# The first MLP block of a fused attention and two-MLP kernel, issued in another order

## The chip, the cores and the metric

The kernel runs on one core of a Trainium2 chip. The metric is the device time of one execution in microseconds (us); lower is better.

## The reference

Delta-rule attention over 768 steps for 4 batches and 8 heads of 48, then a PReLU MLP (384 to 2048 to 384), then a SiLU-gated MLP (384 to 1536 to 384), all on the same 3072 tokens:

```python
for t in range(S):
    y[:, :, t] = np.einsum('bhd,bhde->bhe', q[:, :, t], state)
    v_old = np.einsum('bhde,bhd->bhe', state, kt)          # kt: k / (|k| + 1e-6)
    state = state + bt[..., None] * np.einsum('bhd,bhe->bhde', kt, vt - v_old)
x = y.transpose(0, 2, 1, 3).reshape(B * S, H * D)
h = x @ w_in;  g = np.maximum(h, 0) + alpha * np.minimum(h, 0);  x = g @ w_out
g = x @ w_gate;  out = (g / (1 + np.exp(-g)) * (x @ w_val)) @ w_out2
```

The weights and alpha come as float64.

## The kernel before

The attention is computed in 24 chunks of 32 steps (`NCH`), four chunks to a window. A chunk c goes through six pieces of small products on TensorE: `do_KS` (state against k, tile pk; VectorE then subtracts it from v), `do_QS` (state against q, tile py), `do_U` (tile pu; ScalarE copies U out), `do_S` (the state's update, pst; VectorE adds it to St), `do_Y` (the masked part of the output, added to py; ScalarE copies ys out) and `do_XT` (transposes ys into px; ScalarE and VectorE make xh and xl of it, the high and low parts of the MLP's input). Each of the first five is 64 products of some 32x48 in the profile, most of them 48 columns wide. For each window there is also work ahead: transposes `pre_T` of k and q, small Gram matrices `pre_G` (pg; tiles GL and mt), the mask on mt (`mask_m`, GpSimd), and `lanes`, an elimination in 37 steps on VectorE and GpSimd (L323, L331), which gives the matrix TT that `do_U` reads. `lanes2` does it in another way for window 0.

The first MLP takes blocks n of 64 steps, that is, two chunks, 256 tokens. A block has 16 columns j. `H1` multiplies x with a 128-wide slice of w_in into h (9 products of 128x256, high and low parts), ScalarE and VectorE make pn of it (L692, L693), `H1_parts` splits that into gh (ScalarE L701, GpSimd L702), and `O1` multiplies gh with the slice of w_out into o (9 products). h has two banks of PSUM, so H1 of column j waits for VectorE's pn of column j - 2.

W1, the weights of this MLP, is loaded as float64 and converted while the first block runs. The generator `all_w1` issues the conversion in steps, three to a column: ScalarE scales (`Cut.act`, L592), VectorE does three integer operations (`Cut.dve`, L597, L599, L603), ScalarE rounds to the high part (L887), GpSimd subtracts for the low part (`lo`, L875, twice a column). It also issues the loads of the columns that the prelude hasn't loaded, three columns ahead (`W1_AHEAD`). `mark` writes one element of a tile by ScalarE, so that a load into the tile waits for ScalarE to come there.

Nothing is reordered: each engine runs its instructions in the order in which the program issues them. That order is a list of events. `at(u, fn, ...)` places a piece at the time u, one unit for each column of the first MLP (block n, column j is at 16 n + j), and the list is sorted by u at the end. `prelude` is issued ahead of it and holds chunks 0 and 1. `base(c)` is the place of chunk c. Nearly all DMAs are issued by SyncE, in order, and each waits until the one eight places before it has landed; the W1 loads of columns 7 to 15 are issued by ScalarE, with the same rule.

Of the kernel before, what the change touches and what calls it, by code (L numbers as in the profile page):

```python
# [8 lines left out]
F32 = mybir.dt.float32  # L9
# [15 lines left out]
def kernel(  # L25
# [40 lines left out]
    NB2 = NCH // CB2  # L66
    LA = 2
    W1_DVE = 16
    W1_SP = 7
    W1_AHEAD = 3  # L70
    TURN = 3

# [551 lines left out]
    def load_w1(*slices, eng=nc.sync):  # L624
        for i in slices:
            load_wide(*w1_src(i), w1_64[i // 2][:, i % 2], eng)
# [230 lines left out]
    def at(u, fn, *args):  # L857
        events.append((u, len(events), fn, args))
# [10 lines left out]
    def all_w1():  # L869

        cuts = []

        def lo(p, z0, z1, eng):
            f = cuts[p].f.rearrange("p (a n) -> p a n", a=2)
            eng.tensor_tensor(w1[p][:, z0:z1, 1], f[:, z0:z1], w1[p][:, z0:z1, 0], ALU.subtract)  # L875

        for p in range(J1 + 1):
            while len(cuts) < min(J1, p + (1 if p == 0 else 2)):
                cuts.append(Cut(w1_64[len(cuts)]))
                cuts[-1].act()  # L880
            for z in range(3):
                if p < J1:
                    cuts[p].dve(z)
                if z == 0 and p > 0:
                    w1.append(ws.tile([128, 2, 2, 384], F32R, name="w", tag="w"))
                    f = cuts[p - 1].f.rearrange("p (a n) -> p a n", a=2)
                    nc.scalar.activation(out=w1[p - 1][:, :, 0], in_=f, func=AF.Copy)  # L887
                    lo(p - 1, 0, 1, nc.gpsimd)
                    if p <= W1_DVE:
                        lo(p - 1, 1, 2, nc.gpsimd)  # L890
                if z > 0 and W1_SP <= p + W1_AHEAD < J1:
                    load_w1(2 * (p + W1_AHEAD) + z - 1, eng=nc.scalar)
                if z == 1 and p > W1_DVE:
                    lo(p - 1, 1, 2, nc.vector)
                if p < J1 or z == 1:
                    yield
# [3 lines left out]
    def go(g, n=1):  # L900
        for _ in range(n):
            next(g, None)
# [10 lines left out]
    def prelude():  # L913
# [83 lines left out]
        nc.vector.tensor_scalar(slope[:, 1], slope[:, 1], -1.0, None, op0=ALU.add)  # L997
        nc.vector.tensor_tensor(c, c, slope[:, 1], ALU.mult)
        nc.vector.tensor_scalar(c, c, -1.0, None, op0=ALU.mult)
        go(conv, C_D)  # L1000
        do_Y(1)
        go(conv, 1)
        do_XT(1)
        return inv

    def base(c):
        return {2: 2.9, 3: 7.7, 4: 22.6, 5: 27.2}.get(c, 8 * (c - 2))

    CONV_DONE, CONV_END = 8 + sum(CONVS), 11.0
    CONV_N = 3 * J1 + 1 - CONV_DONE  # L1010
# [2 lines left out]

    for w in range(1, NWIN):
        P = base(4 * w) - 32
        if w == 1:
            for z in range(2):
                at(1.4 + 1.2 * z, lambda: go(inv0[0]))
            for z in range(4):
                at(1.8 + 1.05 * z, pre_T, 1, "q", z // 2, z % 2, nat)  # L1020
            for z in range(4):
                at((5.7, 7.0, 8.8, 10.4)[z], lambda z=z: pre_G(4 + z, raw=True))
                at(13.0 + 2 * z, mask_m, 4 + z)
            for z in range(2):
                at((4.3, 6.4)[z], lambda z=z: pre_G(2 + z, (1,), raw=True))
                at((4.9, 7.5)[z], mask_m, 2 + z)
            l0, l1, n = 10.9, 22.6, LANES
        else:
            if w < TURN:
                at(P - 5, load_nat, w, "k", nat)  # L1030
                for z in range(4):
                    at(P + 1.2 + z, pre_T, w, "k", z // 2, z % 2, nat)
                at(P + 4.5, load_nat, w, "q", nat)
                for z in range(4):
                    at(P + 7.2 + z, pre_T, w, "q", z // 2, z % 2, nat)
            else:
                for z in range(4):
                    at(P - 13 + 1.5 * z, load_split, w, "k", z, nat)
                    at(P - 6.5 + 0.8 * z, turn_T, w, "k", z, nat)
                    at(P - 5.6 + 1.2 * z, load_split, w, "q", z, nat)  # L1040
                    at(P + 3.0 + z, turn_T, w, "q", z, nat)
            at(P - 1, load_beta, w)
            for z in range(4):
                at(P + 11.2 + z, pre_G, 4 * w + z)
            l0, l1, n = P + 15, P + 31.5, LANES
        box = {}

        def step(w=w, box=box):
            if "g" not in box:
                box["g"] = lanes(w, 10)  # L1050
            next(box["g"], None)

        for z in range(n):
            at(l0 + (l1 - l0) * z / n, step)

    at(0.5, do_S, 1)
    at(0.6, load_k2, 2)
    for c in range(2, NCH):
        u = base(c)
        f = {2: 0.8, 3: 0.8, 4: 0.6, 5: 0.6}.get(c, 1.0)  # L1060
        if c > 2:
            at(u - 7, load_v, c)
            at(u - 1.3, load_k2, c)
        at(u - 1.5, scale_v, c)
        at(u + 0.3, do_KS, c)
        at(u + 0.35, do_QS, c)
        at(u + 0.3 + 2 * f, do_U, c)
        at(u + 0.3 + 4 * f, do_S, c)
        at(u + 0.3 + 5 * f, do_Y, c)
        at(u + 0.3 + (7 if c < 4 else 6) * f, do_XT, c)  # L1070
    for n in range(NB1):
        for j in range(J1):
            at(16 * n + j, H1, n, j)
# [78 lines left out]
```

## Time and profile before

| | |
|---|---|
| median of 3 runs | 1093.94 us (1091.84 to 1093.97) |
| the profiled execution | 1094.43 us |
| its span, first to last instruction | 1092.5 us |
| TensorE busy | 1055.2 us (97% of the span), 15649 products |
| VectorE, ScalarE, GpSimd busy | 603.6, 389.9, 359.5 us |
| DMA | 76.34 MB, mean 70 GB/s |

A product shows as busy on TensorE however fast it runs, so the busy share says where TensorE waits, not how fast it is. [...] Idle time of an engine is put down to what ended it; "issue" means that nothing which the profile shows was waited for.

### The profile page before, as it was taken

The numbers are of one execution on the slowest core, as the hardware profiler recorded it, in microseconds if no ns is written. First come the engines' busy times: TensorE is split into PE (matmuls) and PEld (weight loads), VectorE is DVE, ScalarE is ACT, GpSimd is POOL, SyncE is SP. The second block draws the span as 40 slices with busy tenths as digits, with TensorE's granted clock in tenths as the row PEclk, the third lists the DMA queues.
The fourth block names the chain that finished last, engine by engine and source line by source line (L and its number), as shares of the span: only waits on it lengthen the run. The fifth ranks groups of instructions, "written<-read, shape, count | busy, mean of one in ns | idle before, by whom it ended". The sixth has DMA issues, their size and how long they took to land.

```text
span 1092.5 us, 35673 instructions
## 1 busy us (share of the span) xinstructions
PE 1055.2 (97%) x15649; PEld 969.6 (89%) x15649; DVE 603.6 (55%) x1204; ACT 389.9 (36%) x841; POOL 359.5 (33%) x531
## 2 busy tenths in 40 slices
PE   6689899999999999999999999999999999999998
PEld 5588788999999999999999998888888888888887
DVE  5778865975895697489453453433333333333332
ACT  3556343343434334433444653222222222222211
POOL 3478852832563383366333541101001001010000
PEclk9669999999999999999999999999999999999999
DMA  9663042353344236330441541010010010100001
GB/s 196 184 192 105 10 103 53 62 122 95 70 69 134 66 62 139 90 82 11 118 130 56 159 135 54 1 58 1 1 58 1 18 42 1 58 1 1 29 1 29
DMA packets 165979, 76.34 MB, mean 70 GB/s; under 512 B 129824, under 2 KB 160576, under 8 KB 165824
## 3 DMA queue, kind: packets, MB, share of 16 engines
q1 hardware_dynamic: 160256, 66.28, 24.5%
q10 hardware_dynamic: 5184, 7.37, 2.2%
q8 instruction: 122, 2.00, 0.8%
q0 software_dynamic: 384, 0.41, 0.2%
q14 instruction: 33, 0.27, 0.1%
HBM read 57.52 MB, written 16.52 MB: 68 GB/s over the span
## 4 chain that ended last, share of the span: by engine, by line
PE 89%; POOL 4%; issue 2%; DVE 2%; DMA 1%; ACT 1%; SPq 0%; ACTq 0%; POOLq 0%; DVEq 0%
PE gv L772 27%; PE o L713 18%; PE h L682 18%; PE o L802 14%; PE pst L527 2%; PE pg L207 2%; PE pu L506 2%; PE py L548 2%; PE pk L462 2%; PE py L462 1%; POOL w L875 1%; DMA nat<-in_k_dram 1%; POOL gh L702 1%; POOL X L331 1%; POOL tmg L323 1%
## 5 line engine op out<-in xcount | busy, mean ns | idle before, releaser
L772 PE MATMUL gv<-x2s,w 128*128 128x512 f32 x1296 | 307.6, 391 | 0.0
L772 PEld LDWEIGHTS gv<-x2s,w 128*128 128x128 f32 x1296 | 242.5, 188 | 47.8
L713 PE MATMUL o<-gh,w 128*128 128x256 f32 x1728 | 246.2, 288 | 3.9 <-POOL gh L702 3.9
L682 PE MATMUL h<-xh,w 128*128 128x256 f32 x1152 | 241.2, 286 | 3.0 <-DVE pn L693 1.6
L702 POOL TENSOR_TENSOR gh<-pn,gh 128x256 fp32r<-128x256 f32 x192 | 155.3, 809 | 248.5 <-ACT gh L701 217.3
L713 PEld LDWEIGHTS o<-gh,w 128*128 128x128 f32 x1728 | 217.3, 189 | 11.5 <-POOL gh L702 5.1
L682 PEld LDWEIGHTS h<-xh,w 128*128 128x128 f32 x1152 | 192.2, 191 | 5.8 <-DVE pn L693 2.6
L693 DVE SCALAR_TENSOR_TENSOR pn<-pn,slope,h 128x256 f32<-128x256 f32 x192 | 91.3, 476 | 135.9 <-ACT pn L692 135.9
L682 PE MATMUL h<-xl,w 128*128 128x256 f32 x576 | 163.2, 283 | 0.1
L802 PE MATMUL o<-w,us 128*128 128x384 f32 x864 | 162.5, 337 | 0.0
L802 PEld LDWEIGHTS o<-w,us 128*128 128x128 f32 x864 | 151.9, 188 | 7.1 <-DVE os L815 1.4
L692 ACT ACTIVATE pn<-h,slope 128x256 f32<-128x256 f32 x192 | 90.4, 471 | 137.7 <-PE h L682 134.5
L784 DVE TENSOR_TENSOR sg<-sg,gv 128x512 f32<-128x512 f32 x72 | 49.5, 687 | 151.8 <-ACT sg L782 151.7
L701 ACT ACTIVATE gh<-pn 128x256 fp32r<-128x256 f32 x192 | 80.0, 417 | 145.0 <-DVE pn L693 143.2
L682 PEld LDWEIGHTS h<-xl,w 128*128 128x128 f32 x576 | 109.8, 191 | 0.6 <-DVE xl L574 0.6
L757 POOL TENSOR_TENSOR x2s<-x2r,x2s 128x512 fp32r<-128x512 f32 x15 | 19.3, 1320 | 266.6 <-ACT x2s L755 266.6
L789 ACT ACTIVATE us<-u 128x512 fp32r<-128x512 f32 x72 | 45.5, 632 | 171.2 <-DVE u L785 171.2
L782 ACT ACTIVATE sg<-gv 128x512 f32<-128x512 f32 x72 | 43.0, 597 | 159.3 <-PE gv L772 159.3
L790 DVE TENSOR_TENSOR us<-u,us 128x512 fp32r<-128x512 f32 x72 | 49.9, 693 | 54.8 <-ACT us L789 54.8
L785 DVE TENSOR_TENSOR u<-sg,gv 128x512 f32<-128x512 f32 x72 | 49.5, 688 | 49.3 <-PE gv L772 48.8
L331 DVE TENSOR_TENSOR X<-X,tmp 128x31 f32<-128x31 f32 (+29 forms) x155 | 65.0, 419 | 4.8
L323 DVE TENSOR_TENSOR tmp<-L,X 128x31 f32<-128x31 f32 (+29 forms) x155 | 59.5, 384 | 1.8
(120 smaller groups left out, 975.9 us busy)
## 6 DMA issues: line engine op xcount, KB each, us to landing
w<-in_moe_w_out_dram SPq DMA_DIRECT2D x19, 384.0 KB
wf<-w2d SPq DMA_DIRECT2D x36, 192.0 KB
k<-in_k_dram SPq DMA_DIRECT2D x96, 48.0 KB
x2d<-xs SPq DMA_DIRECT2D x12, 384.0 KB
w<-in_moe_w_gate_dram SPq DMA_DIRECT2D x12, 384.0 KB
w<-in_moe_w_val_dram SPq DMA_DIRECT2D x12, 384.0 KB
x2r<-x2d SPq DMA_DIRECT2D x24, 192.0 KB
v<-in_v_dram SPq DMA_DIRECT2D x88, 48.0 KB
```

What stands on the lines that cost most here:

```text
L323: eng.tensor_tensor(w, t.L[:, i + 1:C, i:i + 1].to_broadcast([128, n, m]), t.X[:, i:i + 1, c0:c0 + m].to_broadcast([128, n, m]), ALU.mult,)
L331: eng.tensor_tensor(Xv, Xv, w, ALU.subtract)
L682: nc.tensor.matmul(ps[:, 0:N1], w[:, a, kk * 128:kk * 128 + 128], x[b][:, kk, :], start=(i == 0), stop=(i == 3 * NK - 1),)
L692: nc.scalar.activation(out=g, in_=hv, func=AF.Relu, scale=slope[:, 0, j:j + 1])
L693: nc.vector.scalar_tensor_tensor(out=g, in0=g, scalar=slope[:, 1, j:j + 1], in1=hv, op0=ALU.mult, op1=ALU.add)
L701: nc.scalar.activation(out=gh[:, 0], in_=g, func=AF.Copy)
L702: nc.gpsimd.tensor_tensor(gh[:, 1], g, gh[:, 0], ALU.subtract)
L713: nc.tensor.matmul(o[:, dm // 2, (dm % 2) * N1:(dm % 2) * N1 + N1], w[:, a, dm * 128:dm * 128 + 128], g[:, b], start=(j == 0 and i == 0 an ...
L772: nc.tensor.matmul(p[:, 0:N2], w2[j, z][:, a, kk * 128:kk * 128 + 128], x[:, b, kk], start=(i == 0), stop=(i == 3 * NK - 1),)
L784: nc.vector.tensor_tensor(sg, sg, ps[0], ALU.mult)
L790: nc.vector.tensor_tensor(us[:, 1], u, us[:, 0], ALU.subtract)
L802: nc.tensor.matmul(o2_t[n][t][:, 0:DM], us[:, a, t * 128:t * 128 + 128], w[:, b, :], start=(j == 0 and i == 0), stop=(j == J2 - 1 and i == 2),
```

## The change

All edits concern what is issued up to the end of the second block. In the prelude one conversion step moves behind `do_XT(1)`. The W1 loads of columns 8 to 15 are issued by SyncE, both halves together, each pair behind a `mark`; column 7 is loaded with the prelude's. In the list of events `do_S(1)` moves from 0.5 to 2.45, so that H1 of columns 0, 1 and 2 come first; the rest of window 0's inverse, the transposes of q, the Gram products, the masks and the six pieces of chunks 2 and 3 get places of their own, with `do_KS` and `do_QS` apart; the 37 steps of the elimination of window 1 go from 11.2 to 24.0 in place of 10.9 to 22.6; chunks 4 and 5 start at 24.0 and 28.0 in place of 22.6 and 27.2, with 0.55 columns to a step instead of 0.6.

```diff
--- before.py
+++ after.py
@@ -66,7 +66,7 @@
     NB2 = NCH // CB2
     LA = 2
     W1_DVE = 16
-    W1_SP = 7
+    W1_SP = 8
     W1_AHEAD = 3
     TURN = 3
 
@@ -888,8 +888,10 @@
                     lo(p - 1, 0, 1, nc.gpsimd)
                     if p <= W1_DVE:
                         lo(p - 1, 1, 2, nc.gpsimd)
-                if z > 0 and W1_SP <= p + W1_AHEAD < J1:
-                    load_w1(2 * (p + W1_AHEAD) + z - 1, eng=nc.scalar)
+                if z == 1 and W1_SP <= p + W1_AHEAD < J1:
+                    i = p + W1_AHEAD
+                    mark(w1_64[i].rearrange("p a n -> p (a n)").bitcast(F32)[0:1, 0:1])
+                    load_w1(2 * i, 2 * i + 1)
                 if z == 1 and p > W1_DVE:
                     lo(p - 1, 1, 2, nc.vector)
                 if p < J1 or z == 1:
@@ -997,14 +999,13 @@
         nc.vector.tensor_scalar(slope[:, 1], slope[:, 1], -1.0, None, op0=ALU.add)
         nc.vector.tensor_tensor(c, c, slope[:, 1], ALU.mult)
         nc.vector.tensor_scalar(c, c, -1.0, None, op0=ALU.mult)
-        go(conv, C_D)
         do_Y(1)
-        go(conv, 1)
         do_XT(1)
+        go(conv, C_D + 1)
         return inv
 
     def base(c):
-        return {2: 2.9, 3: 7.7, 4: 22.6, 5: 27.2}.get(c, 8 * (c - 2))
+        return {2: 3.3, 3: 8.3, 4: 24.0, 5: 28.0}.get(c, 8 * (c - 2))
 
     CONV_DONE, CONV_END = 8 + sum(CONVS), 11.0
     CONV_N = 3 * J1 + 1 - CONV_DONE
@@ -1015,16 +1016,16 @@
         P = base(4 * w) - 32
         if w == 1:
             for z in range(2):
-                at(1.4 + 1.2 * z, lambda: go(inv0[0]))
+                at(4.1 + z, lambda: go(inv0[0]))
             for z in range(4):
-                at(1.8 + 1.05 * z, pre_T, 1, "q", z // 2, z % 2, nat)
+                at((3.15, 3.65, 4.65, 5.15)[z], pre_T, 1, "q", z // 2, z % 2, nat)
             for z in range(4):
-                at((5.7, 7.0, 8.8, 10.4)[z], lambda z=z: pre_G(4 + z, raw=True))
+                at((5.6, 6.6, 9.1, 10.6)[z], lambda z=z: pre_G(4 + z, raw=True))
                 at(13.0 + 2 * z, mask_m, 4 + z)
             for z in range(2):
-                at((4.3, 6.4)[z], lambda z=z: pre_G(2 + z, (1,), raw=True))
-                at((4.9, 7.5)[z], mask_m, 2 + z)
-            l0, l1, n = 10.9, 22.6, LANES
+                at((3.1, 8.1)[z], lambda z=z: pre_G(2 + z, (1,), raw=True))
+                at((3.9, 9.4)[z], mask_m, 2 + z)
+            l0, l1, n = 11.2, 24.0, LANES
         else:
             if w < TURN:
                 at(P - 5, load_nat, w, "k", nat)
@@ -1053,21 +1054,19 @@
         for z in range(n):
             at(l0 + (l1 - l0) * z / n, step)
 
-    at(0.5, do_S, 1)
-    at(0.6, load_k2, 2)
+    FIRST = {2: (3.6, 4.6, 6.1, 7.1, 7.6, 8.65), 3: (8.6, 9.6, 10.1, 11.1, 12.1, 12.8)}
+    at(2.45, do_S, 1)
+    at(2.55, load_k2, 2)
     for c in range(2, NCH):
         u = base(c)
-        f = {2: 0.8, 3: 0.8, 4: 0.6, 5: 0.6}.get(c, 1.0)
+        f = {4: 0.55, 5: 0.55}.get(c, 1.0)
         if c > 2:
             at(u - 7, load_v, c)
             at(u - 1.3, load_k2, c)
         at(u - 1.5, scale_v, c)
-        at(u + 0.3, do_KS, c)
-        at(u + 0.35, do_QS, c)
-        at(u + 0.3 + 2 * f, do_U, c)
-        at(u + 0.3 + 4 * f, do_S, c)
-        at(u + 0.3 + 5 * f, do_Y, c)
-        at(u + 0.3 + (7 if c < 4 else 6) * f, do_XT, c)
+        cols = [u + 0.3 + z * f for z in (0, 0.05, 2, 4, 5, 6)]
+        for x, fn in zip(FIRST.get(c, cols), (do_KS, do_QS, do_U, do_S, do_Y, do_XT)):
+            at(x, fn, c)
     for n in range(NB1):
         for j in range(J1):
             at(16 * n + j, H1, n, j)
```

VectorE, from its first pn (L693, which reads an h; h_1025 and h_1128 are columns 0 and 1, w_116 is the float64 W1 of column 6). Before:

```order
L693 SCALAR_TENSOR_TENSOR pn<-pn,slope,h_1025 128x256
L597 TENSOR_SCALAR we<-w_116 128x768
L599 SCALAR_TENSOR_TENSOR w_116<-w_116,we 128x768
L540 COPY St<-pst 128x384
L603 SCALAR_TENSOR_TENSOR w_116<-w_116 128x768
L693 SCALAR_TENSOR_TENSOR pn<-pn,slope,h_1128 128x256
L597 TENSOR_SCALAR we<-w_117 128x768
L599 SCALAR_TENSOR_TENSOR w_117<-w_117,we 128x768
L603 SCALAR_TENSOR_TENSOR w_117<-w_117 128x768
L693 SCALAR_TENSOR_TENSOR pn<-pn,slope,h_1229 128x256
```

In the changed kernel (h_1026, h_1053 and h_1086 are columns 0 to 2):

```order
L693 SCALAR_TENSOR_TENSOR pn<-pn,slope,h_1026 128x256
L597 TENSOR_SCALAR we<-w_116 128x768
L599 SCALAR_TENSOR_TENSOR w_116<-w_116,we 128x768
L603 SCALAR_TENSOR_TENSOR w_116<-w_116 128x768
L693 SCALAR_TENSOR_TENSOR pn<-pn,slope,h_1053 128x256
L597 TENSOR_SCALAR we<-w_117 128x768
L599 SCALAR_TENSOR_TENSOR w_117<-w_117,we 128x768
L603 SCALAR_TENSOR_TENSOR w_117<-w_117 128x768
L693 SCALAR_TENSOR_TENSOR pn<-pn,slope,h_1086 128x256
L597 TENSOR_SCALAR we<-w_118 128x768
L540 COPY St<-pst 128x384
```

The state's copy St of chunk 1 stood behind the first pn; now it stands behind the third, five conversion steps later.

ScalarE, a little further on: before, W1's loads stand among the instructions of columns 1 and 2 (w_119 and w_120 are columns 9 and 10).

```order
L542 ACTIVATE St<-pst 128x384
L608 DMA w_119<-in_moe_w_out_dram 128x384
L692 ACTIVATE pn<-h_1128,slope 128x256
L592 ACTIVATE w_118<-w_118 128x768
L887 ACTIVATE w<-w_116 128x2x384
L423 ACTIVATE tmp<-pi 128x256
L701 ACTIVATE gh<-pn 128x256
L608 DMA w_120<-in_moe_w_in_dram 128x3x128
L190 ACTIVATE kqt<-pt 128x2x4x32 x2
L608 DMA w_120<-in_moe_w_out_dram 128x384
```

In the changed kernel:

```order
L701 ACTIVATE gh<-pn 128x256
L913 ACTIVATE w_120<-mask 1x1
L692 ACTIVATE pn<-h_1086,slope 128x256
L592 ACTIVATE w_119<-w_119 128x768
L887 ACTIVATE w<-w_117 128x2x384
L542 ACTIVATE St<-pst 128x384
L701 ACTIVATE gh<-pn 128x256
L913 ACTIVATE w_121<-mask 1x1
L692 ACTIVATE pn<-h_1195,slope 128x256
```

The loads are gone from ScalarE; a one-element write from the mask stands for each pair.

TensorE where the third block begins (px is chunk 5's transpose, the last input of that block; h_3506 and h_3514 are its column 0). Before:

```order
L682 MATMUL h_3460<-xh,w 128x256
L570 MATMUL px<-ident,ys 128x128 x3
L713 MATMUL o_2553<-gh,w 128x256 x9
L682 MATMUL h_3506<-xh,w 128x256
L682 MATMUL h_3506<-xl,w 128x256
L682 MATMUL h_3506<-xh,w 128x256 x2
L682 MATMUL h_3506<-xl,w 128x256
```

In the changed kernel:

```order
L548 MATMUL py<-U,mt 32x48 x32
L713 MATMUL o_2549<-gh,w 128x256 x9
L570 MATMUL px<-ident,ys 128x128 x3
L682 MATMUL h_3514<-xh,w 128x256
L682 MATMUL h_3514<-xl,w 128x256
L682 MATMUL h_3514<-xh,w 128x256 x2
L682 MATMUL h_3514<-xl,w 128x256
```

The nine products of o stood between px and the block's first h; now they stand ahead of px.

## Rows read from the trace of the kernel before

**Rows 1.** Windows by stage: us, then busy us (xinstructions), granted clock, DMA share, GB/s.
```profile
55.60:110.80 55.20, 50.89 (x1476) 46.57 (x1477) 44.12 (x51) 31.30 (x63) 43.07 (x35) 0.85 0.52 143
118.30:153.80 35.50, 29.97 (x346) 27.51 (x345) 33.82 (x87) 12.24 (x34) 27.48 (x58) 1.00 0.31 63
153.80:187.50 33.70, 32.63 (x933) 29.96 (x931) 13.80 (x30) 14.23 (x36) 7.91 (x10) 1.00 0.23 57
187.50:1092.50 905.00, 899.98 (x11575) 828.58 (x11575) 471.93 (x945) 304.26 (x646) 251.44 (x383) 1.00 0.23 59
```

**Rows 2.** Groups of VectorE, 55.6 to 110.8: busy us, mean ns, idle before and releaser.
```profile
L603 DVE SCALAR_TENSOR_TENSOR w<-w 128x768 int32<-128x768 int32 x11 | 16.6, 1512 | 0.3
L599 DVE SCALAR_TENSOR_TENSOR w<-w,we 128x768 int32<-128x768 int32 x11 | 12.8, 1165 | 0.3
L597 DVE TENSOR_SCALAR we<-w 128x768 int32<-128x768 int32 x10 | 7.4, 741 | 0.0
L693 DVE SCALAR_TENSOR_TENSOR pn<-pn,slope,h 128x256 f32<-128x256 f32 x11 | 5.2, 476 | 6.3 <-ACT pn L692 6.2
```

**Rows 3.** Groups of GpSimd in the same stretch.
```profile
L875 POOL TENSOR_TENSOR w<-w,w 128x384 fp32r<-128x384 f32 x22 | 31.3, 1441 | 14.7 <-ACT w L887 13.9 <-POOL mt L195 0.8
L702 POOL TENSOR_TENSOR gh<-pn,gh 128x256 fp32r<-128x256 f32 x9 | 9.1, 1007 | 0.0
L452 POOL TENSOR_TENSOR v<-v,nn 128x384 f32<-128x384 f32 x2 | 2.7, 1346 | 0.0
L195 POOL TENSOR_TENSOR mt<-mt,mask 128x256 f32<-128x256 f32 x2 | 1.8, 898 | 0.0
```

**Rows 4.** Timeline of VectorE: start, us, instruction, idle before it and releaser.
```profile
53.36 0.95 DVE L603 SCALAR_TENSOR_TENSOR w<-w 128x768 int32<-128x768 int32 x1
54.23 0.55 DVE L597 TENSOR_SCALAR we<-w 128x768 int32<-128x768 int32 x1
55.66 0.56 DVE L574 TENSOR_TENSOR xl<-px,xh 128x384 fp32r<-128x384 f32 x1 [0.88 <-ACT xh L573]
...
66.03 0.55 DVE L597 TENSOR_SCALAR we<-w 128x768 int32<-128x768 int32 x1
...
78.22 1.66 DVE L603 SCALAR_TENSOR_TENSOR w<-w 128x768 int32<-128x768 int32 x1
...
81.83 0.55 DVE L597 TENSOR_SCALAR we<-w 128x768 int32<-128x768 int32 x1
```

**Rows 5.** Timeline of GpSimd.
```profile
42.44 1.99 POOL L875 TENSOR_TENSOR w<-w,w 128x384 fp32r<-128x384 f32 x2 [3.04 <-ACT w L887]
...
62.65 1.45 POOL L702 TENSOR_TENSOR gh<-pn,gh 128x256 fp32r<-128x256 f32 x1
...
79.03 1.45 POOL L702 TENSOR_TENSOR gh<-pn,gh 128x256 fp32r<-128x256 f32 x1
```

**Rows 6.** Timeline of ScalarE.
```profile
65.13 0.48 ACT L692 ACTIVATE pn<-h,slope 128x256 f32<-128x256 f32 x1 [2.55 <-DMA k<-in_k_dram]
```

**Rows 7.** Timeline of TensorE.
```profile
75.32 0.62 PE L462 MATMUL pk<-St,kqt 48*32 48x48 f32 x27 [1.97 <-issue]
...
124.89 0.62 PE L713 MATMUL o<-gh,w 128*128 128x256 f32 x3 [0.63 <-POOL gh L702]
...
185.74 0.49 PE L570 MATMUL px<-ident,ys 128*128 128x128 f32 x3
...
187.13 0.28 PE L682 MATMUL h<-xh,w 128*128 128x256 f32 x1
187.51 0.39 PE L682 MATMUL h<-xl,w 128*128 128x256 f32 x1
```

**Rows 8.** Chain that ended last, 146 to 150: start, us, what.
```profile
147.58 1.06 PE h L682 x9
148.65 1.06 PE o L713 x9
```

**Rows 9.** Groups of VectorE, 118.3 to 153.8.
```profile
L693 DVE SCALAR_TENSOR_TENSOR pn<-pn,slope,h 128x256 f32<-128x256 f32 x12 | 5.6, 470 | 0.0
```

## The prediction

> **What bounds the kernel now.** I read the stage windows first, then the groups of instructions of VectorE and GpSimd in the first stretch that is not full, then the timelines around its holes. From 187.5 us on TensorE is busy for 900.0 of 905.0 us [rows 1]: that part moves as a block, and what the change is worth is what it does ahead of it. There are three stages. [...] In the second (118.3 to 153.8, the elimination of window 1) VectorE is nearly full, 33.8 of 35.5 us, and TensorE idles for 5.5 us [rows 1]. In the third (153.8 to 187.5) TensorE is full but for 1.1 us [rows 1].
>
> **Stage 1: what the new order can give back.** VectorE idles for 55.2 - 44.1 = 11.1 us. That isn't all to be had, because VectorE's conversions and GpSimd's subtractions hold each other up: the third conversion (L603) takes 0.95 us when GpSimd is idle and 1.66 when it isn't [rows 4]; two subtractions of L875 take 1.99 us alone [rows 5], 1.0 each, and 1.44 each on the mean of this stage [rows 3]. So I count a shared resource. GpSimd's share is what its instructions take alone: 22 of L875 at 1.0, 9 of L702 at 0.67 (an estimate from their size, 256 elements for 384), 2 of L452 at 1.0 and 2 of L195 at 0.67, by size again, together 31.4 us [rows 3]. VectorE's share is what a blocked L603 takes beyond the one subtraction of 1.0 that it lets by: 1.66 - 1.0, near 0.7. With 22 of L603 and L599 at 0.7 and 10 of L597 at some 0.35 (an estimate: half, as its 0.55 alone stands to 0.95) that is 18.9 us [rows 2, 4]. Sum 50.3 of 55.2 us: at most 4.9 are free.
>
> Two holes in which neither engine uses it show in the timelines. The first runs from 64.10 (end of GpSimd's 62.65 + 1.45) to 66.03 (VectorE's next L597): 1.9 us [rows 4, 5]. Its cause is ScalarE, which stood 2.55 us for a DMA before it took up the pn of column 1 at 65.13 [rows 6]: its next instruction but for that was the issue of a W1 load. In the changed kernel ScalarE issues no W1 load, and column 1 follows column 0 directly on TensorE. The second runs from 80.48 (79.03 + 1.45) to 81.83: 1.35 us [rows 4, 5]. It goes back to TensorE, which stood 1.97 us for its own instructions in the middle of the 64 small products of pk, with the 64 of py right behind [rows 7], so that column 4 came late. In the changed order the first three columns run ahead and pk and py lie a column apart. I take both holes as regained: -3.3 us.
>
> Against it: two conversions (L603 at 53.36, 0.95 us, and L597 at 54.23, 0.55) ran while VectorE waited for the second x tile; they now stand behind its xl [rows 4]. The xl moves up from 55.66 by the 0.88 us that it waited, to 54.8; with 0.5 for it, 0.9 and 0.55 the next L599 starts near 56.85 and not at 56.14: +0.7 us [rows 4]. **Stage 1: -2.6 us.** Its bounds are +0.7 (no hole closes) and -8 us: VectorE's whole idle time would be -11.1 + 0.7, but GpSimd's 43.1 us have to fit too, with some 4 us for its hand-overs.
>
> [...]
>
> The other edits of this stage cost nothing that I can find. SyncE now has the W1 loads of columns 8 to 15 among its k, v and q loads, each behind a one-element mark of ScalarE. The marks add a 1x1 ScalarE instruction to eight columns in place of two DMA issues, on an engine that is busy for 31.3 of 55.2 us [rows 1]. In SyncE's order the marks of columns 10 and 11 come before chunk 2's k load, which waits for the first pst; that wait ends before ScalarE reaches the mark of column 12. If it did not, a load would come late for a conversion that follows its mark by nearly two columns, some 8 us: that is the cover. The state copy (L540) stands two columns later on VectorE, and pk waits for it; TensorE has the columns in hand to lie idle there.
>
> **Stage 2: -1.5 us.** The elimination's 37 steps are spread over 12.8 columns (11.2 to 24.0) and not 11.7 (10.9 to 22.6). VectorE is the bound, so the stretch grows by 1.1 columns' worth of its pn, 0.47 each [rows 9], or of GpSimd's gh at 0.67 to 0.75; but TensorE gets 1.1 more columns done inside it, 1.06 + 1.06 = 2.1 us each [rows 8], which it then needn't do behind. 1.1 x (2.1 - 0.75) = 1.5 us. Bounds: 0, if the steps bunch as before, and -2.5.
>
> **Stage 3: +0.9 us.** Chunk 5's transpose px was followed by nine products of o before the third block's first h. Now o stands ahead of px and h right behind it. Before, px ended at 185.74 + 0.49 = 186.23 and the second product of h, which wants xl, started at 187.51: 1.28 us for the hop over ScalarE and VectorE [rows 7]. Bare of its cover it costs 1.28 less the first product, 0.12 (nine take 1.06 [rows 8]), less the 0.26 by which it already showed (the first two products start 0.38 apart and not 0.12): 0.9 us. Bounds 0.5 and 1.3. That chunks 4 and 5 start later and run at 0.55 columns a step instead of 0.6 I put at nothing, since TensorE had no wait for them; a rival takes it up.
>
> **Sum.** -2.6 - 1.5 + 0.9 = -3.2 us. The profiled execution took 1094.43 us (span 1092.5), so 1091.2; it lies 0.5 above the median of the runs, 1093.94. Forecast: 1090.8 us.
>
> **Rivals.**
> Every wait goes. If the two engines overlap better than my count, stage 1 gives its -8 us: -8 - 1.5 + 0.9 from 1093.94 is 1085.3. For it: with TensorE three columns ahead, none of VectorE's 6.3 us before pn [rows 2] has a reason left. Against it: L875 already runs at 1.44 for 1.0 [rows 3], and filling holes makes that worse.
> [...]
> Slower: the tight run of chunks 4 and 5. Each has five hand-overs between TensorE, VectorE and ScalarE (pk, pu, pst, py, px) in a stretch in which TensorE has nothing to spare. A hand-over that comes late cost 0.63 us where the trace has one, before the product of o at 124.89 [rows 7]. Ten of them would be 6.3 us: 1097.1. It decides from the fifth on, since 5 x 0.63 = 3.2. Against it: at 0.6 columns a step none was late.
> The change does nothing where it says most: W1 issued by SyncE alone may have been hidden but for the one wait of 2.55 us; then the gain is that of the order alone, and it lies in the forecast's own range.
>
> **How the numbers follow.** 4.2 in 10 for the forecast (1088.5 to 1092.5 by its own bounds), 2.2 for every wait gone, 2.2 for the full port, 1.4 for the slower one. About 0.2% (2.2 us) is what a measurement of this kernel can tell from no change: faster means below 1091.75. Of the forecast 4.0 lie there or near it and 0.2 within; all of the second; the third is 2.0 within and 0.2 slower; the fourth 0.1 within and 1.3 slower. Faster 0.62, same 0.23, slower 0.15. The range leaves out the far end of the first rival and most of the slower one: 1085.5 to 1095.
>
> **What would show it.** Right: no ScalarE wait for a DMA between 58 and 70 us; VectorE's idle time from the first h to the last L603 well under 11 us, and L603's mean above its 1.51 [rows 2]; TensorE's idle time in the elimination under 5.5 us; a wait near 1.2 us at the first h of the third block. Wrong: L603 and L875 longer by as much as VectorE's waits are shorter; ScalarE waiting for a W1 load; TensorE waiting at pk, pu, pst or py of chunks 4 and 5; or new waits of TensorE for its own instructions, which I can't place.

## The result, and the profile after

The changed kernel takes 1105.18 us (median of 6 runs, 1099.23 to 1106.38), the kernel before 1092.42 us in the same comparison (6 runs, 1091.84 to 1093.97). The ratio is 1.010, with a 95% interval of 1.0074 to 1.0125: slower, where the forecast was 1090.8 us and its range ended at 1095. The profiled execution took 1105.27 us with a span of 1103.5, which is 11.0 more than before.

The stage windows of the changed kernel, cut at the places that answer to [rows 1] (the first block beside W1's conversion, the elimination, chunks 4 and 5, the rest); busy us by engine, then the granted clock (the share of its full speed that TensorE was granted), DMA share and GB/s:

```profile
57.80:112.20 54.40, 46.21 (x1407) 41.58 (x1407) 46.15 (x53) 33.71 (x71) 42.85 (x34) 0.92 0.51 144
118.30:154.20 35.90, 30.55 (x303) 29.08 (x302) 34.00 (x88) 13.02 (x37) 27.88 (x58) 1.00 0.32 62
154.20:196.60 42.40, 36.75 (x1060) 33.92 (x1059) 18.23 (x39) 14.58 (x38) 9.53 (x14) 0.91 0.20 50
196.60:1103.50 906.90, 902.06 (x11575) 830.90 (x11575) 469.92 (x943) 304.15 (x645) 249.17 (x382) 0.99 0.23 59
```

The rest takes 906.9 us against 905.0: it did move as a block. The third window is where the time went: 42.4 us for 33.7, TensorE idle for 5.6 us in place of 1.1, and the granted clock 0.91 in place of 1.00. The first two give nothing back. The same is seen from the first product of h of some columns, read from TensorE's timeline of both kernels:

```
                          before   changed   difference
block 1, column 0          55.68     57.82      +2.1
block 2, column 8         153.81    154.13      +0.3
block 2, column 12        170.02    170.36      +0.3
block 2, column 13        174.61    178.98      +4.4
block 2, column 15        184.67    189.11      +4.4
block 3, column 0         187.13    195.57      +8.4
block 3, column 1         191.31    203.19     +11.9
block 3, column 2         193.44    205.32     +11.9
```

At column 12 the changed kernel still has chunk 5's pk and py ahead of it, 1.6 us of products that the kernel before has done by then, so it is 1.9 behind, no more than the 2.1 that its prelude was late. From there to the end two things happen. The timeline of TensorE shows them:

```profile
176.16 0.79 PE L462 MATMUL py<-St,kqt 48*32 48x48 f32 x26 [2.08 <-issue]
...
195.57 0.39 PE L682 MATMUL h<-xh,w 128*128 128x256 f32 x1 [2.83 <-ACT xh L573]
196.62 0.58 PE L682 MATMUL h<-xl,w 128*128 128x256 f32 x1 [0.67 <-DVE xl L574]
```

The first is a stall of 2.08 us in the middle of chunk 5's py, put down to "issue". The second is the hop from px to the third block's h: 2.83 us for xh and 0.67 for xl, where [rows 7] has 0.26. What is late there is read from VectorE's timeline of the same stretch:

```profile
191.28 0.42 DVE L223 TENSOR_TENSOR mt<-pg,mask 128x256 f32<-128x256 f32 x1 [4.30 <-PE py L548]
191.62 0.35 DVE L597 TENSOR_SCALAR we<-w 128x384 int32<-128x384 int32 x1
191.89 1.01 DVE L538 TENSOR_TENSOR St<-pst,St 128x384 f32<-128x384 f32 x2
192.82 0.55 DVE L599 SCALAR_TENSOR_TENSOR w<-w,we 128x384 int32<-128x384 int32 x1
193.29 1.03 DVE L269 STREAM_TRANSPOSE L<-GL 128x512 f32<-128x512 f32 x1
194.24 0.44 DVE L693 SCALAR_TENSOR_TENSOR pn<-pn,slope,h 128x256 f32<-128x256 f32 x1
...
195.07 1.06 DVE L269 STREAM_TRANSPOSE L<-GL 128x512 f32<-128x512 f32 x1
196.05 0.52 DVE L574 TENSOR_TENSOR xl<-px,xh 128x384 fp32r<-128x384 f32 x1
```

VectorE stands for 4.30 us at the mask of the last Gram products (`pre_G`, L223, tile mt), which waits for chunk 5's masked products py (mt has six buffers, and the code makes a new mask wait for the products that read an old one; a seventh was not tried). Those were moved behind column 15's h. The kernel before has the same wait, 2.04 us long, but it ends before column 15's h is ready:

```profile
183.67 0.42 DVE L223 TENSOR_TENSOR mt<-pg,mask 128x256 f32<-128x256 f32 x1 [2.04 <-PE py L548]
```

In the changed kernel a conversion step, the sums of St, another step and a transpose of 1.03 us come next behind the mask, and only then, at 194.24, the pn of column 15, whose h was ready at 190.3. ScalarE takes its instructions in order, so gh and xh come after that pn:

```profile
194.72 0.42 ACT L701 ACTIVATE gh<-pn 128x256 fp32r<-128x256 f32 x1 [3.01 <-DVE pn L693]
195.04 0.47 ACT L573 ACTIVATE xh<-px 128x384 fp32r<-128x384 f32 x1
```

Both waits cost twice. The granted clock, windows behind each of them:

```profile
176.00:182.00 6.00, 5.84 (x82) 5.49 (x84) 0.29 (x1) 0.47 (x1) 0.00 (x0) 0.50 0.01 3
196.00:202.00 6.00, 5.38 (x139) 5.04 (x140) 4.49 (x12) 1.15 (x3) 1.89 (x3) 0.51 0.29 70
```

Behind the 2.08 us stall the granted clock is 0.50, and behind the idle 3.5 us 0.51, where [rows 1] has 1.00 for both stages of the kernel before. From column 0 to column 1 of the third block it then takes 7.62 us and not 4.18: of these 3.4 us, 0.7 are the wait for xl, and 2.8 come behind it, at the lower clock (from the second product of h to column 1, 6.57 us for 3.80).

The first block, VectorE's groups from the first column to the last conversion (compare [rows 2]), and its timeline in columns 1 and 2:

```profile
L603 DVE SCALAR_TENSOR_TENSOR w<-w 128x768 int32<-128x768 int32 x12 | 16.9, 1411 | 0.3
L599 DVE SCALAR_TENSOR_TENSOR w<-w,we 128x768 int32<-128x768 int32 x11 | 13.8, 1257 | 0.3
L597 DVE TENSOR_SCALAR we<-w 128x768 int32<-128x768 int32 x11 | 8.4, 761 | 0.0
L693 DVE SCALAR_TENSOR_TENSOR pn<-pn,slope,h 128x256 f32<-128x256 f32 x11 | 5.2, 474 | 5.1 <-ACT pn L692 5.1
```

```profile
62.70 0.98 DVE L597 TENSOR_SCALAR we<-w 128x768 int32<-128x768 int32 x1
63.72 1.67 DVE L599 SCALAR_TENSOR_TENSOR w<-w,we 128x768 int32<-128x768 int32 x1
65.42 1.66 DVE L603 SCALAR_TENSOR_TENSOR w<-w 128x768 int32<-128x768 int32 x1
```

VectorE has no wait at all from 57.80 to 84.4 us: the two holes are closed, and no wait of ScalarE for a load of 2.55 us is left (the longest is 0.67 us). But the conversions run blocked, 0.98, 1.67 and 1.66 us where they take 0.55, 0.96 and 0.95 while GpSimd is idle (L597 and L603 in [rows 4], L599 at 59.73 us in this trace). Then new holes open, because TensorE comes late:

```profile
73.16 1.12 PE L185 MATMUL pt<-ident,nat 128*128 128x128 f32 x4 [2.44 <-DVE St L540]
...
82.66 0.80 PE L462 MATMUL py<-St,kqt 48*32 48x48 f32 x56 [1.13 <-issue]
...
87.45 0.78 PE L430 MATMUL pi<-tmp,Dm 16*32 16x16 f32 x70 [1.73 <-issue]
```

The transposes wait 2.44 us for the copy of St that the prediction let stand two columns later at no cost, and the small products of chunk 2 stall for 1.13 and 1.73 us; VectorE then waits for pn and for pi (1.32, 2.09, 2.39 and 1.41 us between 84 and 98). From column 0 to column 10 the first block takes 52.3 us against 52.1. Single traces scatter here: in this trace and those of the seven runs below that are built on the changed kernel and do all its work, it takes 51.6 to 54.1 us, 52.8 on the mean; in the trace of before and those of the seven runs built on it that leave W1's subtractions and the instruction count alone, 49.2 to 52.1 us, 50.9 on the mean. So the new order gains nothing in this stage, and it rather loses.

### The profile page after: what moved, and what is told of

Same layout as the page of the kernel before. It is cut to its first block, busy times and chain, and to the rows that moved or that the text cites. A ratio compares the mean times of both kernels' runs of the same rounds, so it can differ in the third digit from the quotient of the medians.

```text
span 1103.5 us, 35688 instructions
## 1 busy us (share of the span) xinstructions
PE 1054.4 (96%) x15649; PEld 969.6 (88%) x15649; DVE 603.8 (55%) x1204; ACT 391.6 (35%) x849; POOL 358.6 (32%) x531
## 4 chain that ended last, share of the span: by engine, by line
PE 91%; issue 3%; POOL 3%; DVE 3%; DMA 0%; ACT 0%; SPq 0%; POOLq 0%; DVEq 0%; ACTq 0%
PE gv L772 27%; PE o L713 19%; PE h L682 18%; PE o L802 14%; PE pg L207 2%; PE pst L527 2%; PE pu L506 2%; PE py L548 2%; PE pk L462 2%; PE py L462 2%; PE px L570 1%; POOL X L331 1%; POOL tmg L323 1%; PE pt L185 1%; POOL gh L702 0%
## 5 line engine op out<-in xcount | busy, mean ns | idle before, releaser
L713 PEld LDWEIGHTS o<-gh,w 128*128 128x128 f32 x1728 | 218.8, 190 | 11.1 <-POOL gh L702 3.9
L693 DVE SCALAR_TENSOR_TENSOR pn<-pn,slope,h 128x256 f32<-128x256 f32 x192 | 91.1, 475 | 144.0 <-ACT pn L692 140.1
```

The source lines that it names most:

```text
L693: nc.vector.scalar_tensor_tensor(out=g, in0=g, scalar=slope[:, 1, j:j + 1], in1=hv, op0=ALU.mult, op1=ALU.add)
L713: nc.tensor.matmul(o[:, dm // 2, (dm % 2) * N1:(dm % 2) * N1 + N1], w[:, a, dm * 128:dm * 128 + 128], g[:, b], start=(j == 0 and i == 0 an ...
```

## The experiments

Each ratio is against runs of the kernel before on the same chip, with its 95% interval.

**Which half loses.** Chunks 4 and 5 and the elimination put back in the changed kernel, and their new places alone in the kernel before:

```diff
-        return {2: 3.3, 3: 8.3, 4: 24.0, 5: 28.0}.get(c, 8 * (c - 2))
+        return {2: 3.3, 3: 8.3, 4: 22.6, 5: 27.2}.get(c, 8 * (c - 2))
-            l0, l1, n = 11.2, 24.0, LANES
+            l0, l1, n = 10.9, 22.6, LANES
-        f = {4: 0.55, 5: 0.55}.get(c, 1.0)
+        f = {4: 0.6, 5: 0.6}.get(c, 1.0)
```

> The changed kernel with only chunks 4 and 5 and the 37 elimination steps put back to their old places (10.9 to 22.6; 22.6 and 27.2; 0.6 columns a step). Theory A, the loss is made where chunk 5 meets the third block: all of it goes, 1091 to 1095 us against 1092.4 before. Theory B, the loss is made in the first block (its new order, W1's loads) and only shows later: 1098 us or more.

> The kernel before with only the new places of chunks 4 and 5 and of the elimination steps; W1's loads and the first block's order stay old. Theory A: the whole loss, 1101 to 1107 us. Theory B: at most 3 us slower than before, up to 1095.5.

With them put back: 1.0007 (0.9995 to 1.002), 1095.81 us, a little above theory A's 1095. With them alone: 1.0084 (1.0071 to 1.0097), 1102.79 us. Theory A holds: nearly the whole loss is made by the new places of chunks 4 and 5. The first block's new order with W1's new route can't be told from nothing in this time, beside the old places of chunks 4 and 5; beside other places it can (see the last pair under "All cures together"). TensorE's waits of the second one are those of the changed kernel:

```profile
174.33 0.53 PE L462 MATMUL py<-St,kqt 48*32 48x48 f32 x27 [2.07 <-issue]
...
192.50 0.38 PE L682 MATMUL h<-xh,w 128*128 128x256 f32 x1 [2.83 <-ACT xh L573]
```

**The hold at the mask.** Chunk 5's masked products moved ahead of the last Gram products in the changed kernel (`at(30.15, do_Y, 5)`), and, in the kernel before, behind column 15 and o as in the changed one (`at(31.05, do_Y, 5)`, `at(31.6, do_XT, 5)`):

> The changed kernel with chunk 5's masked products (py of do_Y) issued 0.9 columns earlier, ahead of the last Gram products pg, whose mask on VectorE waits 4.30 us for them; px stays behind o. Theory W, VectorE stands at that mask and the state's sums, a transpose and the pn of column 15 pile up behind it, so that ScalarE's gh and xh are late: the wait goes, px to h falls from 2.83 to about 1.3 us, the clock holds, 5 to 7 us less than the changed kernel (1098 to 1100). Theory H, it is the bare hop px, xh, xl, h alone: 0 to 2 us less.

> The kernel before with one edit: chunk 5's masked products and px issued behind column 15 and o, as in the changed kernel; the state's sums stay ahead of the mask on VectorE. Theory W: VectorE stands some 4 us at the mask, the pn of column 15, gh and xh are late, 3 to 6 us slower than before. Theory H, only the bare hop: 0.5 to 1.5 us slower.

The first gives 1.006 (1.0041 to 1.0079), 1100.45 us: 4 thousandths less than the changed kernel, with intervals that just overlap. VectorE's wait at the last mask is 1.24 us and no longer for py, and xh is waited for 0.58 us, not 2.83:

```profile
186.19 0.42 DVE L223 TENSOR_TENSOR mt<-pg,mask 128x256 f32<-128x256 f32 x1 [1.24 <-ACT GL L217]
```

```profile
175.54 0.79 PE L462 MATMUL py<-St,kqt 48*32 48x48 f32 x26 [2.36 <-issue]
...
187.93 1.22 PE L713 MATMUL o<-gh,w 128*128 128x256 f32 x8 [0.83 <-issue]
...
192.18 0.38 PE L682 MATMUL h<-xh,w 128*128 128x256 f32 x1 [0.58 <-ACT xh L573]
```

The second gives 1.0034 (1.002 to 1.0048), 1098.5 against 1094.18 us. VectorE stands 3.20 us at the mask, the pn of column 15 comes at 183.76, TensorE waits 2.03 us for xh, and the granted clock is 0.70 from 185 to 190 and 0.62 from 190 to 195:

```profile
181.60 0.42 DVE L223 TENSOR_TENSOR mt<-pg,mask 128x256 f32<-128x256 f32 x1 [3.20 <-PE py L548]
...
183.76 0.44 DVE L693 SCALAR_TENSOR_TENSOR pn<-pn,slope,h 128x256 f32<-128x256 f32 x1
```

```profile
185.08 0.39 PE L682 MATMUL h<-xh,w 128*128 128x256 f32 x1 [2.03 <-ACT xh L573]
```

Theory W is borne out from both sides: the second time as expected (3 to 6 us slower), the first just outside (1098 to 1100 us). In the first run the stall in py stays (2.36 us), and a new one of 0.83 us stands behind py, pg and pst, which are now in a row.

**The stall.** Chunk 5's py behind o in the changed kernel (`at(28.6, do_QS, 5)`), and ahead of o, directly behind pk, in the kernel before (`at(u + 0.3, do_QS, 5)`):

> The changed kernel with chunk 5's py products (state against q) half a column later, behind the nine products of o, so that no more than 128 small products (pg, pk) stand in a row instead of 192. If the 2.08 us stall in the middle of those 64 py products and the lower clock behind it come from the run of small products: 3 to 5 us less than the changed kernel, 1100 to 1102. If that stall falls anywhere (it goes by what else is loaded then) or its time is idle elsewhere anyway: within 1.5 us of the changed kernel.

> The kernel before with one edit: chunk 5's py products directly behind pk, ahead of o, so that pg, pk and py stand as 192 small products in a row, as in the changed kernel. If the run of small products makes TensorE stall for its own instructions: a stall of 1.5 to 2.5 us inside py, and 1.5 to 4.5 us slower than before with the lower clock. If the stall in the changed kernel came from something else: within 1 us of before.

```profile
174.38 0.61 PE L462 MATMUL py<-St,kqt 48*32 48x48 f32 x35 [0.72 <-issue]
...
190.70 0.38 PE L682 MATMUL h<-xh,w 128*128 128x256 f32 x1 [2.84 <-ACT xh L573]
```

The first gives 1.0076 (1.0059 to 1.0093), 1101.33 us, less than the changed kernel by the medians, though the two intervals overlap: the stall falls from 2.08 to 0.72 us (and 0.35 in pu), the clock stays at 1.00 from 170 to 186, and the hold at the mask is untouched (2.84 us). The second falsified my reason for it: pg, pk and py stand in a row without any wait, and the time is that of before, 1.0002 (0.9992 to 1.0012):

```profile
165.66 1.10 PE L207 MATMUL pg<-kqt 48*32 48x64 f32 x64
166.58 0.86 PE L462 MATMUL pk<-St,kqt 48*32 48x48 f32 x64
167.26 0.86 PE L462 MATMUL py<-St,kqt 48*32 48x48 f32 x64
```

So 192 small products in a row don't stall by themselves. Next I moved one chunk alone in the kernel before: chunk 5 to 28.0 with 0.55, or the elimination and chunk 4 to 24.0 with 0.55:

> The kernel before with chunk 5 alone at its new place (28.0, 0.55 columns a step); chunk 4 and the elimination stay. Theory R, the row pg, pk, py of chunk 5 with o ahead of px is what costs: a stall near 2 us inside py, the hold at the mask and the late xh, 7 to 10 us slower than before. Theory D, the stall comes from two chunks' products in fewer columns: under 1 us of stall inside py, the hold and the late xh alone, 3 to 6 us slower.

> The kernel before with the elimination over 11.2 to 24.0 and chunk 4 alone at its new place (24.0, 0.55); chunk 5 stays at 27.2, so that the two chunks follow each other still closer. Theory R: no stall over 1 us in chunks 4 and 5, and the wider elimination's 1.5 us show, 1 to 2 us faster than before. Theory D: stalls of together 1.5 us or more in chunks 4 and 5, within 1.5 us of before or slower.

```profile
170.43 0.53 PE L462 MATMUL py<-St,kqt 48*32 48x48 f32 x27 [1.21 <-issue]
```

```profile
168.20 0.38 PE L462 MATMUL pk<-St,kqt 48*32 48x48 f32 x5 [3.20 <-issue]
```

Chunk 5 alone: 1.0065 (1.0046 to 1.0084), a stall of 1.21 us, between the two theories, with hold and late xh as in the changed kernel. Chunk 4 alone: 1.0022 (1.0009 to 1.0036), a stall of 3.20 us inside chunk 5's pk, where neither kernel has one. Theory D has the sign, but neither says where a stall falls. Counting TensorE's instructions in the traces does (weight loads, products and queue instructions in their order of time): of the 278 rows between 9 and 210 us that put an idle time of TensorE down to "issue", in the traces of the two kernels and of the other 17 runs, 255 lie 193 or 194 behind a multiple of 256, and the other 23 are of 0.66 us or less, at two fixed places of the prelude. The profile shows such blocks on the DMA side too: the pages of both kernels list 122 packets of the kind "instruction" on queue q8, 2.00 MB, and TensorE's 15649 products and 15649 weight loads in the kernel before are 122.3 times 256. Whether a stall follows goes largely by how fast the block of 256 instructions ahead of it was used up, counted from one such place to the next: behind the first h, in the traces of the two kernels and of all 18 runs, a stall (over 0.15 us) followed 80 of the 113 blocks that took under 3 us, 49 of the 214 of 3 to 5 us, and 1 of the 194 longer ones. The block that ends in chunk 5's py takes 1.44 us in the changed kernel; in the kernel before the block with the same number takes 4.09 us and no stall follows. The last run moves the whole program against that count:

```diff
             nc.tensor.matmul(warm_t[0][0:96, 0, 0:96], t, t, start=True, stop=True)
+        for _ in range(56):
+            nc.tensor.matmul(warm_t[0][0:32, 0, 0:16], t[0:32, 0:32], t[0:32, 0:16], start=True, stop=True)
```

> The kernel before with 56 tiny products (32x16) more behind the first warming ones, where TensorE waits for the first load anyway; they show as 112 products, 224 instructions with their weight loads. Theory B, TensorE gets its instructions in blocks of 256 and stalls where it has used one up faster than the next comes: the stalls stay 193 to 196 behind a multiple of 256 and so fall at other products (none inside chunk 2's pk or chunk 5's py), and those behind the first product of h shrink from 5.1 us together to about 2, since fewer blocks there hold nothing but small products: 2 to 5 us faster than before. Theory S, the stalls belong to certain pieces of the program: they stay inside pk and py, within 1 us of before.

```profile
63.61 0.53 PE L408 MATMUL pi<-TT,GL 32*32 32x16 f32 x42 [1.22 <-issue]
...
68.92 0.73 PE L430 MATMUL pi<-tmp,Dm 16*32 16x16 f32 x64 [0.93 <-issue]
...
78.56 0.53 PE L207 MATMUL pg<-kqt 48*32 48x32 f32 x37 [0.65 <-issue]
...
87.34 0.32 PE L207 MATMUL pg<-kqt 48*32 48x32 f32 x14 [0.60 <-issue]
...
91.26 0.54 PE L207 MATMUL pg<-kqt 48*32 48x64 f32 x24 [0.54 <-issue]
```

The places are as theory B has them: all of these stay 193 or 194 behind a multiple of 256 and fall at other products, pk and py of chunk 2 have 0.25 us at most, chunk 5 has none. Its gain isn't there: 1.001 (1.0001 to 1.0019). The profiled execution was the fastest of 12 (1089.54 us, with a median of 1094.05), so these rows are of a run better than most. Nor did the stalls behind the first h fall as far as expected: together they are 4.2 us, for 5.1 before and some 2 expected.

**All cures together.** py apart and masked products early; with px ahead of column 15 too (`at(30.95, do_XT, 5)`); with pst ahead of column 14 besides (`at(29.95, do_S, 5)`); and these places in the kernel before:

> The changed kernel with both edits: chunk 5's py (state against q) behind the nine products of o, and its masked products ahead of the last Gram products. If the two losses stand apart, as the traces with one edit each say (the stall at 4.3 us, the hold at 6), the gains add up: 1093 to 1096 us. If one loss only takes the other's place: 1098 or more.

> The same, with chunk 5's transposes px moved ahead of the column 15's products as well, so that o and a whole column cover the hop px, xh, xl. If the bare hop is worth the 0.9 us that the prediction gave it: 0.7 to 2 us below the kernel with both edits. If px now waits for ys instead: no gain.

> The changed kernel with five places of chunk 5 altered so that no more than 128 small products stand in a row, the masked products come ahead of the last Gram products, and px a column ahead of the third block: py behind o, the state's products ahead of column 14, the masked products behind it, px ahead of column 15. Theory: stalls inside runs of 192 small products, the hold at the mask and the bare hop are all that the changed kernel loses. Then it is at the kernel before or up to 3 us faster, 1090 to 1094 us. If each stall that is taken away comes back elsewhere: 1096 or more.

> The same places of the elimination and of chunks 4 and 5 in the kernel before, whose W1 loads and first block stay old. If the new first block is worth nothing: the same as the run above within 1.5 us. If the elimination's wider spread is worth the 1.5 us of the prediction: 1 to 3 us faster than before.

1.0051 (1.0032 to 1.007), 1.0023 (1.0007 to 1.0038), 1.0043 (1.0031 to 1.0055) and 1.0000 (0.9988 to 1.0012). The gains don't add up: with both cures a stall of 1.46 us stands where there was none,

```profile
187.06 1.21 PE L713 MATMUL o<-gh,w 128*128 128x256 f32 x8 [1.46 <-issue]
```

and px a column earlier is worth some 3 us more by the medians (1096.2 against 1099.35 us, where 0.7 to 2 were expected; the two intervals just overlap). Nothing here beats the kernel before.

The last two differ only in the prelude, the first block and W1's route, and they are 4.3 thousandths apart, with intervals that don't overlap, where 1.5 us was the bound for a new first block that is worth nothing. So beside these places the new first block costs time. Of the 3.4 us between their profiled executions, 2.1 stand ahead of the first h (58.16 and 56.02 us) and the rest behind it; no run separates the order from the prelude here.

**The first block.** W1's loads by SyncE alone in the kernel before; column 7 out of the prelude again (`W1_SP = 7` in the first kernel of this section):

> The kernel before with only W1's loads by SyncE, both halves behind a mark, and column 7's with the prelude. If ScalarE's 2.55 us wait for a DMA held up the first block: 1 to 2 us faster than before (1091 to 1093). If the wait only delays work that the shared resource of VectorE and GpSimd would have delayed anyway: within 1 us of before.

> The kernel with chunks 4 and 5 put back (first block and W1's loads of the changed kernel), but column 7 of W1 loaded behind its mark in the first block and not in the prelude. If column 7's load in the prelude delays TensorE's instructions there: the longest stall of the prelude falls from 3.4 to about 2.4 us, the first product of h comes 1 us earlier, and the time is 0.5 to 1.5 us lower than with it. If that stall only varies from run to run: no difference.

1.0012 (0.9998 to 1.0025) and 1.0003 (0.999 to 1.0016). The wait of ScalarE for the DMA was worth nothing: without it the first of these takes 52.1 us from column 0 to column 10, as before. The prelude's pk (L475) has a stall of 4.73 us in the changed kernel,

```profile
46.52 0.86 PE L475 MATMUL pk<-U,mx 32*32 32x48 f32 x32 [4.73 <-issue]
```

and of 1.99 with column 7 taken out. It varies by itself: 2.8 to 4.7 us in the nine traces with column 7 in the prelude, 1.7 to 3.9 in ten without. On the mean it is 3.6 and 2.5 us, which points at column 7's loads, but the first h comes only 0.7 us later (57.0 and 56.4 us on the mean), and in the time of the two kernels with and without it no difference can be measured.

What holds the first block: the kernel with chunks 4 and 5 put back without `lo` (the low part of W1 is left out, and as many products read the high part twice), and the kernel before with half or all of `lo` on VectorE from the seventh column on, with all work done (`W1_DVE = 6`; for all, the other `lo` too on `nc.vector`):

> The kernel with chunks 4 and 5 put back, without GpSimd's 32 subtractions for W1's low part (the products read the high part twice, so part of the computation is left out; as many products). Theory P, the conversions of VectorE and GpSimd's subtractions hold each other up and that sets the first block's pace: VectorE's third conversion step falls from 1.4 to about 0.96 us, and the time by 4 us or more against the same kernel with them. Theory T, TensorE's own stalls and clock set it: less than 2 us.

> The kernel before, with the second of the two subtractions of each column of W1 (from the seventh column converted on) on VectorE and not GpSimd. Theory P, the engines hold each other up: VectorE's three conversion steps fall from 3.4 us a column on the mean by 0.5 or more, which pays for its 0.55 us subtraction, 0 to 2 us faster than before. Theory V, VectorE's amount of work sets the pace: 10 x 0.55 us more work, 2 to 5 us slower.

> The same with both subtractions on VectorE. Theory P: the conversion steps run at nearly their times alone (0.95, 0.96, 0.55), and what they lose less (about 1 us a column) is what the two subtractions cost (1.1): within 2 us of before. Theory V: 10 x 1.1 us more work on VectorE, 5 to 10 us slower.

```profile
L603 DVE SCALAR_TENSOR_TENSOR w<-w 128x768 int32<-128x768 int32 x12 | 12.9, 1074 | 0.3
L599 DVE SCALAR_TENSOR_TENSOR w<-w,we 128x768 int32<-128x768 int32 x11 | 11.0, 1004 | 0.3
L597 DVE TENSOR_SCALAR we<-w 128x768 int32<-128x768 int32 x11 | 6.9, 623 | 0.0
```

```profile
L875 DVE TENSOR_TENSOR w<-w,w 128x384 fp32r<-128x384 f32 x16 | 11.1, 693 | 2.7 <-ACT w L887 2.5
L599 DVE SCALAR_TENSOR_TENSOR w<-w,we 128x768 int32<-128x768 int32 x9 | 10.3, 1142 | 0.0
L603 DVE SCALAR_TENSOR_TENSOR w<-w 128x768 int32<-128x768 int32 x8 | 8.7, 1094 | 0.0
L597 DVE TENSOR_SCALAR we<-w 128x768 int32<-128x768 int32 x9 | 4.9, 549 | 0.0
```

Without the subtractions: 0.9971 (0.9956 to 0.9986) against 1.0007 with them, 3.9 us less by the ratios, but some 2 to 6 with their intervals, so that neither theory P (4 or more) nor theory T (less than 2) is settled by the time; the steps still take 1.07, 1.00 and 0.62 us. With half on VectorE: 1.0002 (0.9993 to 1.0011), and the three steps take 3.02 us a column for 3.48 in the same window (62 to 108 us) of before, but a subtraction takes 1.28 us there and not the 0.55 that theory P had for it, near the 0.56 of xl, of the same shape [rows 4]. With all: 1.0011 (0.9999 to 1.0023). In the last one VectorE does 11.1 us of subtractions more between 62 and 108 us, and its conversions give 6.2 of that back: in the same window of before the three steps took 13.3, 9.9 and 6.9 us (1.48, 1.23 and 0.76 each) for as many of them. Theory V is out, and moving this work between the two engines is neutral in time: some of what VectorE has more to do comes back in shorter conversions, and part of the rest took the place of waits.

## Why the prediction was wrong, by its own steps

**The step that failed** is the sentence that put the later start of chunks 4 and 5 and their 0.55 columns a step "at nothing, since TensorE had no wait for them". It costs nearly the whole loss: 1.0084 alone, of 1.010 (with the wider elimination). I asked who waits for these products on TensorE and not who waits on VectorE: the mask of the last Gram products needs chunk 5's masked products, and the pn of the column that TensorE needs next stands behind it. In the kernel before that wait was there too (2.04 us), with an end that came early enough; the prediction's words against the slower rival, that none was late at 0.6 columns a step, looked at TensorE alone.

**The slower rival** had the sign and the place but the wrong price: not ten hand-overs at 0.63 us, but one hold of 4.30 us on an engine that was idle, one stall of 2.08 us, and a granted clock of 0.51 and 0.50 behind them. It had 1.4 in 10. The forecast's own 1088.5 to 1092.5 does not follow from the bounds of its terms, which add up to 1083.9 to 1095.9 us; the result lies outside of both. For the 4 us of GpSimd's hand-overs in one of these bounds there is no row.

**Stage 3, +0.9 us for the bare hop.** The mechanism was right and is seen bare with both cures, 0.58 + 0.67 = 1.25 us, that is 1.0 more than the 0.26 of before. In the changed kernel it was 6.6 us (column 15 to column 1 takes 14.08 us for 6.64, and 0.8 of the difference are the masked products, which now stand there): 3.8 of them up to the second product of h, since xh waited for a pn that the hold had delayed, and 2.8 behind it for the clock.

**Stage 1, -2.6 us.** The two holes did close: VectorE idles for 54.4 - 46.15 = 8.3 us between the first column and the last conversion, where it was 11.1, though 1.5 of these 2.8 us are only the two conversion steps that now stand inside the stretch. The step that failed is the one from there to TensorE: the forecast took time regained on VectorE for time regained by the columns, and column 10 comes 52.3 us behind column 0, for 52.1, with a mean over traces that is 1.9 us worse than with the old order. In columns 1 to 5 the conversions are blocked throughout (L603 takes 1.31 to 1.68 us), and behind them TensorE's own waits set the pace, among them the one for the St copy, which I had put at nothing too (2.44 us). The mark that I gave, L603 above 1.51 us, is wrong: it is 1.41, and the three steps together take 3.43 us a column, for 3.42 before. So this stage gains nothing, as the prediction had it for its full port (2.2 in 10), but not by conversions that got longer: on the mean they did not. No run shows a port; what the traces show is that the conversions take longer while GpSimd works beside them, L603 1.66 us for 0.95 [rows 4], and that without GpSimd's subtractions it takes 1.07 on the mean. How the lost gain divides between that and TensorE's waits was bounded only: all that GpSimd's subtractions cost is 3.9 us (some 2 to 6).

**Stage 2, -1.5 us.** The wider elimination does bring column 8 of the second block 26.1 us behind its column 0, for 28.0 before, also in the run with the new places alone. But 1.6 of these 1.9 us are chunk 4's pk and py, which come later now and are paid for behind. Net, 0.3.

**The prelude** was left out of the sum. In the profiled execution it is 2.1 us longer; its stalls vary that much from run to run, and on the mean of the traces the first h comes 0.7 us later with column 7's loads, less than it scatters.

**What stays open.** Stalls for instructions stand at fixed counts and mostly follow blocks that are used up fast, but their sizes (nothing to 3.2 us at such places beside the MLP) were not explained, and the kernel whose trace has 0.9 us less of them behind the first h (4.2 for 5.1) has no lower median. In the run of all cures on the changed kernel 4.3 thousandths are left, and none in the same places on the kernel before: why the new first block costs more there than the 1.0007 beside the old places is open.

## What to carry to other kernels

When a group of work is moved later, look on every engine for instructions that were already waiting for it, and list what stands behind them in that queue: a wait that costs nothing on an idle engine (2.04 us before) becomes the longest one (4.30) as soon as a column that TensorE needs is queued behind it. An idle time of TensorE in a full stretch can cost more than itself: behind the 2.08 us here the granted clock was 0.50 for some 6 us (nine products of o took 2.29 us in it and 1.34 behind it), while behind one of 1.46 us, with both cures, it stayed at 1.00. And a hole between two engines whose instructions lengthen each other (L603 1.66 us for 0.95 here) is not a gain until the longer instructions beside it are counted.

## What the runs showed of the hardware

TensorE's stalls for its own instructions lie at one place in blocks of 256 instructions: 255 of 278 rows are 193 or 194 behind a multiple of 256, in the traces of 19 kernels, and they fall at other products when 224 instructions are put ahead. The 122 packets of the kind "instruction" fit the same blocks (122.3 of them). With 64-product pieces of some 0.9 us a stall takes up to 3.2 us beside the MLP, and 4.73 in the prelude. That the next block comes too late there was not shown; it is the author's theory B. The runs show the places, and that stalls follow short blocks (80 of 113 under 3 us, 1 of 194 over 5), but not the wait for a packet itself.
